# Attention and top-1 mixture of experts: written order on every engine, fixed weight buffers, later small loads, first unit loaded tile by tile

## Chip, cores and metric

The kernel runs on one core of one Trainium2 chip, in one launch. The metric is the device time in microseconds (us); of several runs it is the median. Engines are named as in the profile: PE (TensorE matmul), PEld (its weight load), DVE (VectorE), ACT (ScalarE), POOL (GpSimd), SP (SyncE, which here only issues DMAs).

## What is computed

Four batches of channel attention (a 256 x 256 softmax matrix per batch, taken over 3648 rows), and then every row goes to one of 16 experts, chosen by two argmax steps.

```
qn = q / (norm(q, axis=1) + 1e-6);  kn = k / (norm(k, axis=1) + 1e-6)     # B=4, N=3648, C=256
s = kn.transpose(0, 2, 1) @ qn / tau;  a = softmax(s, -1)                  # 256 x 256
x = (v @ a).reshape(B * N, C)                                              # 14592 rows
g_idx = argmax(x @ w_group);  e_idx = argmax(x @ w_expert[g_idx])          # 4 groups of 4 experts
out = (g_weight * e_weight) * (relu(x @ w1[g, e]) @ w2[g, e])              # F = 1024
```

## The kernel before

**Attention units.** A batch's 3648 rows are cut into 28 tiles of 128 rows and one of 64, and these into 8 units: seven of four tiles and a short one of one tile (`rows_of`, L150), so there are 32 units in all. An S unit adds its q and k tiles to the score matrix (`s_mm`, L193): three tiles as plain fp32 matmuls, the fourth (`SPLIT`) as three matmuls of rounded parts made by `s_split` (L167). `s_split` also squares the raw rows on ACT, and `s_add` (L186) adds the squares up on DVE. When a batch's S units are done, the generator `softmax` (L211) makes the attention matrix times [identity, routing weights], as two rounded parts `ahi`, `alo`. An X unit transposes four v tiles on PE (`x_tr`, L275), rounds them into `th` (ACT) and `tl` (DVE), and multiplies them (`x_mm`, L289); ACT copies the result to `xs`, DVE the 20 routing logits to `L`.

**Routing.** `routing` (L317) turns the logits of a range of tiles into slots, mostly on DVE with two small PE matmuls (`pp`). `scatter` (L391) has POOL write each tile's rows to their slots in device memory (`x_sorted`) with an indirect DMA, 116 of them, each followed by a small POOL memset (`pause`). X rows wait for this in a ring of `RING` = 10 buffers, which `xg` rows share.

**Experts.** 28 items of 512 rows of one expert each (`ffn1`, `ffn2`, L787 to L810; 8 steps an item, `lag` 2). The first `KPRE` = 4 items are full blocks found early, from the rows of batches 0 and 1 and the first 20 tiles of batch 2 (`PRE`); the others need the whole routing and its tables. The last 24 items also host small blocks ("q", L866 to L925). Weights come through three rotating buffers of one tag (`raw_tile`, L598) and are split into two rounded parts on ACT and DVE.

**Order.** The tile framework's scheduler orders instructions on each engine, with priorities given by hand (`high_priority` at L633, L707, L711). POOL goes by program order from the start (L622); all engines do from the 33rd step of the attention loop (L724) to the second expert step (L1022); then only SP and POOL. The attention loop (L721) runs S unit t beside X unit t - 10. q, k, v and the weights come on SP's queue; `tau` and the routing weights are five small DMAs on ACT's queue, issued first (L89 to L96). The first S unit comes in two halves (L162).

Of the kernel before, what the change touches and what calls it, by code (L numbers as in the profile page):

```python
# [17 lines left out]
P = 128  # L18
B, NT, C = 4, 3648, 256
N = B * NT  # L20
E = 16
# [16 lines left out]
KPRE = 4  # L38
# [5 lines left out]
RANGES = [[(0, 16), (16, NJ)], [(0, 16), (16, NJ)], [(0, 16), (16, 20), (20, NJ)], [(0, 16), (16, NJ)]]  # L44
# [8 lines left out]
XOFF = GPB + 2  # L53
TM = US
TURNS = (0, 1, 2, 3)
# [3 lines left out]
def attention_moe(ctx: ExitStack, tc, q, k, v, tau, w_group, w_expert, w1, w2, out):  # L59
# [29 lines left out]
    ACT.dma_start(tauc, tau[0:1, 0:1].broadcast_to([P, 1]))  # L89
    rtau = cp.tile([P, 1], F32, name="rtau")  # L90
    DVE.reciprocal(rtau, tauc)
    wcat = cp.tile([P, 2, NL], F32, name="wcat")
    for c in range(2):
        ACT.dma_start(wcat[:, c, 0:4], w_group[c * P:(c + 1) * P, :])
        ACT.dma_start(wcat[:, c, 4:NL].rearrange("p (g e) -> p g e", g=4),
                     w_expert[:, c * P:(c + 1) * P, :].rearrange("g p e -> p g e"))  # L96
# [9 lines left out]
    scms = {}  # L106
    for n in {j1 - j0 for r in RANGES for j0, j1 in r}:
        scms[n] = cp.tile([P, E * n], F32, name=f"scm{n}")
        DVE.memset(scms[n], 1.0)
        DVE.memset(scms[n].rearrange("p (e j) -> p e j", e=E)[:, :, 0:1], 0.0)  # L110
    carry = cp.tile([P, E], F32, name="carry")
    DVE.memset(carry, 0.0)
# [19 lines left out]
    DVE.tensor_tensor(part, part, slot1, ALU.add)  # L132
    zero = cp.tile([P, RW], F32, name="zero")
# [8 lines left out]
    vp = vp_.enter_context(tc.tile_pool(name="vp", bufs=3, side="right"))  # L142
# [15 lines left out]
    def s_load(u):  # L158
        rows, nj = rows_of(u % GPB)
        raw = spool.tile([P, 2, GJ, C], F32, tag="raw", name="qkraw", bufs=LOADS + 1)  # L160

        for j0, j1 in ((0, 2), (2, nj)) if u == 0 else ((0, nj),):  # L162
            for i, src in ((0, q), (1, k)):
                SP.dma_start(raw[:rows, i, j0:j1, :], tiles_of(src, u // GPB, u % GPB)[:, j0:j1, :])
        su[u] = dict(raw=raw)

    def s_split(u):  # L167
# [4 lines left out]
        if g < NG:  # L172
# [4 lines left out]
        if g == 0:  # L177
            d["acc"] = ps.tile([P, 2, C], F32, tag="acc", name="sacc")
            d["sqa"] = spool.tile([P, 2, GJ, C], F32, tag="sqa", name="sqa", bufs=1)
            ACT.activation(d["sqa"], raw, AF.Square)  # L180
        else:
            sq = spool.tile([P, 2, GJ, C], F32, tag="sq", name="sq")
            ACT.activation(sq[:rows, :, :nj, :], raw[:rows, :, :nj, :], AF.Square)  # L183
            x["sq"] = sq

    def s_add(u):  # L186
        b, g = divmod(u, GPB)
        if g:
            rows, nj = rows_of(g)
            sqa = st[b]["sqa"]  # L190
            DVE.tensor_tensor(sqa[:rows, :, :nj, :], sqa[:rows, :, :nj, :], su[u]["sq"][:rows, :, :nj, :], ALU.add)  # L191

    def s_mm(u):  # L193
# [3 lines left out]
        for j in range(nj):  # L197
            if j == SPLIT:
                hi, lo = x["hi"], x["lo"]
                terms = (hi, hi), (hi, lo), (lo, hi)  # L200
            else:
                t = x["raw"][:, :, j, :]
                terms = (t, t),
            for c in range(2):
                cs = slice(c * P, (c + 1) * P)
                for kt, qt in terms:
                    PE.matmul(d["acc"][:, c, :], kt[:rows, 1, cs], qt[:rows, 0, :],  # L207
                              start=d.pop("first", True) and c == 0, stop=(g == NG), skip_group_check=True)
                    d["first"] = False

    def softmax(b):  # L211

        d = st[b]
        ssq = ap_.tile([P, 2, C], F32, name="ssq", bufs=1)
# [3 lines left out]
        PE.matmul(nps[:, 0:C], onesf, ssq[:, 0, :], start=True, stop=False, skip_group_check=True)  # L218
        for c in range(2):
            PE.matmul(nps[:, C + c:C + c + 1], ssq[:, 1, c * P:(c + 1) * P], onesf[:, 0:1],  # L220
                      start=False, stop=True, skip_group_check=True)
        yield
        rn = ap_.tile([P, C + 2], F32, name="rn", bufs=1)
        ACT.activation(rn, nps[:, 0:C + 2], AF.Sqrt)
        DVE.tensor_scalar(rn, rn, 1e-6, None, ALU.add)
        DVE.reciprocal(rn, rn)
        DVE.tensor_scalar(rn[:, C:C + 2], rn[:, C:C + 2], rtau, None, ALU.mult)
        sm = ap_.tile([P, 2, C], F32, name="sm", bufs=1)
        for c in range(2):
            DVE.scalar_tensor_tensor(sm[:, c, :], d["acc"][:, c, :], rn[:, C + c:C + c + 1], rn[:, 0:C],  # L230
                                     ALU.mult, ALU.mult)
        mx = ap_.tile([P, 2], F32, name="mx")
        DVE.tensor_reduce(mx, sm, AX.X, ALU.max, negate=True)
        yield
        se = ap_.tile([P, 2], F32, name="se")
        for c in range(2):
            ACT.activation(sm[:, c, :], sm[:, c, :], AF.Exp, bias=mx[:, c:c + 1], accum_out=se[:, c:c + 1])
        DVE.tensor_scalar(se, se, 1e-9, None, ALU.add)
# [4 lines left out]
        yield  # L243
        yield
# [4 lines left out]
        yield  # L249
        aT = ap_.tile([P, 2, C], F32, name="aT", bufs=1)  # L250
        ACT.activation(aT.rearrange("p c n -> p (c n)"), atp, AF.Copy)
        yield
        yield
# [5 lines left out]
        yield  # L259
        DVE.tensor_copy(ax[:, :, C:NE], awp[:, 0:2 * NL].rearrange("p (c n) -> p c n", c=2))  # L260
        ahi = ap_.tile([P, 2, NE], F32R, name="ahi")
# [913 lines left out]
```

## Time and profile before

| | us |
|---|---|
| three runs | 963.89, 962.31, 960.90 (median 962.31) |
| profiled execution, its own time | 958.63 |
| its span, first to last instruction | 956.9 |
| outside the span | 1.73 |
| granted TensorE clock, mean | 0.994 |

The profile is one execution, 3.7 us under the median of the runs. Views give start times from the span's start. PE's busy time is modelled from its instructions, so two matmuls in a pipeline overlap in it; what a piece of PE work takes is read from the distance between starts.

### The profile page before, as it was taken

What the parts mean: (1) busy time and instruction counts of PE and PEld (TensorE: products, weight loads), DVE (VectorE), ACT (ScalarE), POOL (GpSimd) and SP (SyncE); (2) the same over time, 40 slices, a digit from 0 to 9 for tenths busy, and PEclk for the clock granted to TensorE, in tenths of its full rate; (3) what the DMA queues carried; (4) which work ended last, traced back from release to release, by engine and by line L of the source; (5) the groups of instructions that cost most, each with busy time, mean ns of one, the idle gap of its engine ahead of it and who ended that gap; (6) DMA issues with size and microseconds to landing.
All of it is one profiled execution on the core that took longest, in us unless ns stands there. A gap on an engine that the chain in (4) does not pass through costs nothing.

```text
span 956.9 us, 17625 instructions
## 1 busy us (share of the span) xinstructions
PE 924.3 (97%) x6238; PEld 809.5 (85%) x6238; DVE 750.0 (78%) x1511; ACT 477.3 (50%) x748; POOL 332.2 (35%) x425
## 2 busy tenths in 40 slices
PE   7999999988899999999999999999999999999995
PEld 6889899878799988888888888888888888888884
DVE  6989978798899977777877777778777877887731
ACT  6777768447554444444444444444443444444421
POOL 0003878878787322222111311232223222322121
PEclk9999999999999999999999999999999999999998
DMA  8866778448684545555566555666666666556500
GB/s 314 313 243 224 238 269 295 144 147 287 202 296 153 176 159 210 208 210 211 213 219 212 202 213 204 222 229 221 222 223 230 222 222 220 197 212 211 200 25 26
DMA packets 105585, 201.90 MB, mean 211 GB/s; under 512 B 10035, under 2 KB 64059, under 8 KB 105488
## 3 DMA queue, kind: packets, MB, share of 16 engines
q1 hardware_dynamic: 89056, 156.12, 47.6%
q0 software_dynamic: 14944, 44.54, 12.1%
q8 instruction: 51, 0.84, 0.3%
q14 instruction: 46, 0.38, 0.1%
q10 hardware_dynamic: 1488, 0.02, 0.1%
HBM read 170.33 MB, written 31.39 MB: 211 GB/s over the span
## 4 chain that ended last, share of the span: by engine, by line
PE 80%; DVE 6%; POOL 4%; issue 4%; DMA 2%; ACT 2%; POOLq 0%; SPq 0%; DVEq 0%; ACTq 0%
PE yacc L809 32%; PE hmm L793 32%; PE sacc L207 7%; POOL x_sorted L405 3%; PE qacc L913 2%; PE qmm L896 2%; PE xmm L303 2%; DMA qkraw<-in_k 2%; DVE sqa L191 1%; POOL pad L139 1%; PE vtr L284 1%; DMA x_sorted<-xs,si 1%; DVE vtl L286 1%; ACT sq L183 1%; PE qtr L903 1%
## 5 line engine op out<-in xcount | busy, mean ns | idle before, releaser
L797 ACT ACTIVATE hh<-hmm 128x512 fp32r<-128x512 f32 x224 | 133.4, 596 | 298.0 <-PE hmm L793 284.5
L819 POOL DMA_INDIRECT out<-ys,ids x112 | 111.1, 992 | 479.1 <-ACT ys L816 449.1
L809 PE MATMUL yacc<-wh,hh 128*128 128x256 f32 x896 | 256.2, 286 | 0.1
L809 PE MATMUL yacc<-wh,hl 128*128 128x256 f32 x896 | 252.5, 282 | 0.0
L809 PE MATMUL yacc<-wl,hh 128*128 128x256 f32 x896 | 252.0, 281 | 0.0
L798 DVE SCALAR_TENSOR_TENSOR hl<-hmm,hh 128x512 fp32r<-128x512 f32 x224 | 153.4, 687 | 85.9 <-ACT hh L797 84.3
L809 PEld LDWEIGHTS yacc<-wh,hh 128*128 128x128 f32 x896 | 168.7, 188 | 24.4 <-issue 15.0
L793 PE MATMUL hmm<-xth,wh 128*128 128x512 f32 x448 | 177.3, 396 | 0.0
L793 PE MATMUL hmm<-xth,wl 128*128 128x512 f32 x448 | 177.0, 395 | 0.0
L793 PE MATMUL hmm<-xtl,wh 128*128 128x512 f32 x448 | 176.8, 395 | 0.0
L809 PEld LDWEIGHTS yacc<-wl,hh 128*128 128x128 f32 x896 | 169.0, 189 | 8.2
L687 DVE STREAM_TRANSPOSE xt<-xg 32x256 f32<-32x256 f32 x384 | 167.2, 435 | 6.5 <-DMA xg<-x_sorted,ix_big 0.2
L640 DVE TENSOR_TENSOR wl<-wraw,wh 128x1024 fp32r<-128x1024 f32 x112 | 134.9, 1223 | 46.9 <-ACT wh L639 45.6
L809 PEld LDWEIGHTS yacc<-wh,hl 128*128 128x128 f32 x896 | 168.5, 188 | 0.0
L405 POOL DMA_INDIRECT x_sorted<-xs,si x116 | 135.6, 1169 | 56.3 <-issue 29.3
L639 ACT ACTIVATE wh<-wraw 128x1024 fp32r<-128x1024 f32 x112 | 116.2, 1055 | 74.1 <-DMA wraw<-in_moe_w 50.5
L793 PEld LDWEIGHTS hmm<-xth,wl 128*128 128x128 f32 x448 | 84.1, 188 | 19.9
L793 PEld LDWEIGHTS hmm<-xtl,wh 128*128 128x128 f32 x448 | 84.2, 188 | 11.0 <-DVE xtl L668 0.3
L793 PEld LDWEIGHTS hmm<-xth,wh 128*128 128x128 f32 x448 | 84.2, 188 | 9.7
L207 PE MATMUL sacc<-qkraw 128*128 128x256 f32 (+1 forms) x352 | 85.2, 388 | 6.0 <-DMA qkraw<-in_k 6.0
L207 PEld LDWEIGHTS sacc<-qkraw 128*128 128x128 f32 (+1 forms) x352 | 65.0, 193 | 14.6 <-DMA qkraw<-in_q 5.9
L303 PE MATMUL xmm<-ahi,vth 128*128 128x276 f32 (+1 forms) x232 | 69.7, 302 | 3.2 <-ACT ahi L263 1.8
(233 smaller groups left out, 1212.3 us busy)
## 6 DMA issues: line engine op xcount, KB each, us to landing
wraw<-in_moe_w SPq DMA_DIRECT2D x56, 1024.0 KB, 7.2
wraw<-in_moe_w SPq DMA_DIRECT2D x96, 512.0 KB, 5.4
vr<-in_v SPq DMA_DIRECT2D x28, 512.0 KB, 4.2
qkraw<-in_q SPq DMA_DIRECT2D x27, 512.0 KB, 4.8
qkraw<-in_k SPq DMA_DIRECT2D x27, 512.0 KB, 5.7
xg<-x_sorted SPq DMA_DIRECT2D x4, 544.0 KB, 4.0
x_sorted<-xs,si POOLq DMA_INDIRECT x116, 4.0
out<-ys,ids POOLq DMA_INDIRECT x112, 3.6
```

Of the source, the lines that this page charges most:

```text
L207: PE.matmul(d["acc"][:, c, :], kt[:rows, 1, cs], qt[:rows, 0, :], start=d.pop("first", True) and c == 0, stop=(g == NG), skip_group_check= ...
L303: PE.matmul(mm[:rows, :NE], vt[:, c, j * P:j * P + rows], at[:, c, :], start=(n == 0), stop=(n == 5))
L405: ins = POOL.indirect_dma_start(out=xs_d, out_offset=bass.IndirectOffsetOnAxis(ap=si[:rows, j:j + 1], axis=0), in_=xs[:rows, t, 0:RW].bitc ...
L639: ACT.activation(whs[n][:, s], raw[:, s], AF.Copy)
L640: DVE.tensor_tensor(wls[n][:, s], raw[:, s], whs[n][:, s], ALU.subtract)
L687: ins = DVE.transpose(xt[qs_, :, :, rs], xg[:, :, :, qs_])
L793: PE.matmul(mm, wt[:, c, fs], xt[:, c, :], start=(n == 0), stop=(n == 5))
L797: d["hh"] = ACT.activation(hh, mm, AF.Relu)
L798: d["hl"] = DVE.scalar_tensor_tensor(hl, mm, 0.0, hh, ALU.max, ALU.subtract)
L809: PE.matmul(a, ht[:, tsl], wt[:, f, :], start=(f == 0 and t % 2 == 0 and n == 0), stop=(f == 7 and n == 2), skip_group_check=True)
L819: ins = POOL.indirect_dma_start(out=out, out_offset=bass.IndirectOffsetOnAxis(ap=d["ids"][:, t:t + 1], axis=0), in_=ys[:, t, :], in_offset ...
L896: PE.matmul(mm[r, :], qs["xT"][q % 2][:, c, r], qs["w", p][:, c * 512:(c + 1) * 512], start=(c == 0), stop=(c == 1), tile_position=(0, p * ...
```

## The change

On all engines the program's order holds from the first attention unit to the end of the expert loop. Steps are cut finer and interleaved by hand: S and X tiles alternate, squares and their sums come in halves, `softmax` and `routing` yield a number of "hooks" (one hook after each tile) before they go on, and `take`/`give` keep two users of one PSUM buffer apart. X starts at unit 13 instead of 10, with two extra X-only steps (`ALONE`). The sum of squares ends in two additions instead of a reduction; the norms are 4 columns instead of 258 and are spread by a diagonal matmul; the copy of logits and part of the score scaling move from DVE to ACT; units 9 to 12 are not split. `KPRE` is 3 and `PRE` 16 tiles, batch 2 has three routing ranges. Weight buffers have fixed tags, the expert loop's DVE and ACT pieces follow a table (`PLAN`), and output scatters are held back until the fourth item's rows are asked for. `tau` and routing weights are loaded on SP at step 2, and the first unit comes as tile 0, tile 1, tiles 2 and 3, with q on SP and k on ACT.

```diff
-KPRE = 4
+KPRE = 3
+FLIP = 4
...
-RANGES = [..., [(0, 16), (16, 20), (20, NJ)], ...]
+RANGES = [..., [(0, 8), (8, 16), (16, NJ)], ...]
-PRE = (2, 20)
+PRE = (2, 16)
+VLOADS = 3
+UNSPLIT = (9, 10, 11, 12)
+FIRST = GPB + 5
+ALONE = (13, 15)
+HOP = 4
...
-    ACT.dma_start(tauc, tau[0:1, 0:1].broadcast_to([P, 1]))
...
+    def small_loads():
+        SP.dma_start(tauc, tau[0:1, 0:1].broadcast_to([P, 1]))
+        for c in range(2):
+            SP.dma_start(wcat[:, c, 0:4], ...)
+            SP.dma_start(wcat[:, c, 4:NL]..., ...)
...
-        for j0, j1 in ((0, 2), (2, nj)) if u == 0 else ((0, nj),):
+        for j0, j1 in ((0, 1), (1, 2), (2, nj)) if u == 0 else ((0, nj),):
             for i, src in ((0, q), (1, k)):
-                SP.dma_start(raw[:rows, i, j0:j1, :], ...)
+                (ACT if u == 0 and i else SP).dma_start(raw[:rows, i, j0:j1, :], ...)
...
-        DVE.tensor_reduce(ssq, d["sqa"].rearrange("p t j c -> p t c j"), AX.X, ALU.add)
-        yield
+        DVE.tensor_tensor(sqa[:, :, 0:2, :], sqa[:, :, 0:2, :], sqa[:, :, 2:4, :], ALU.add)
+        DVE.tensor_tensor(ssq, sqa[:, :, 0, :], sqa[:, :, 1, :], ALU.add)
+        yield hop
+        ACT.activation(tmp1, onesf[:, 0:1], AF.Sqrt)
+        while not take():
+            yield 1
...
+        ACT.activation(rn, nps[:, C:C + 4], AF.Sqrt)
+        ACT.activation(tmp1, zero[:, 0:1], AF.Exp)
...
-        DVE.tensor_copy(d["L"][:rows, g * GJ:g * GJ + nj, :], xs[:rows, :nj, C:NE])
+            ACT.activation(d["L"][:rows, g * GJ:g * GJ + nj, :], xs[:rows, :nj, C:NE], AF.Copy)
...
-    def raw_tile():
-        return wp.tile([P, 2048], F32, tag="wraw", name="wraw", bufs=3)
+    def raw_tile(n=None):
+        n = turn[0] % 3 if n is None else n
+        turn[0] += 1
+        return wp.tile([P, 2048], F32, tag=f"wraw{n}", name="wraw", bufs=1)
...
-        d[which + "r"] = t = raw_tile().rearrange("p (c f) -> p c f", c=n)
+        d[which + "r"] = t = raw_tile(0 if turn[0] > 9 else None).rearrange("p (c f) -> p c f", c=n)
...
-    ms.enter_context(tc.manual_schedule(engines={ET.Pool}))
+    ms.enter_context(tc.manual_schedule(engines={ET.Pool, ET.SP, ET.Activation, ET.PE, ET.DVE}))
...
+    def hook():
+        hooks[0] += 1
+        small.hook()
+        rgens.hook()
...
+    for n, (t, x) in enumerate(steps):
...
+        if n == 2:
+            small_loads()
...
+        if x == UX - 4:
+            while wp is None:
+                hook()
+            fetch_x(items[0], tb_pre, 0)
+        while x is not None and pend_of(x - RING + (x >= UX - 4)):
+            hook()
+            scatter(2)
...
+        for j in range(GJ):
+            if t is not None and j < rows_of(t % GPB)[1]:
+                s_tile(t, j)
...
+                hook()
+            if j == 0 and nx is not None:
+                x_tr(nx, 1)
+                hook()
+            if x is not None and j < rows_of(x % GPB)[1]:
+                x_tile(x, j)
+                hook()
...
+            if j == 1 and x == UX - 2:
                 split_x(items[0])
...
-        t = raw_tile()
+        t = raw_tile(1 + half)
...
+    PLAN = {(0, 0): range(0, 2), (0, 1): range(2, 4), (1, 0): ("w1", 0), (2, 0): ("w1", 1), (2, 1): range(4, 7),
+            (3, 0): range(7, 9), (3, 1): range(9, 12), (4, 0): range(12, 14), (4, 1): range(14, 16),
+            (5, 0): ("w2", 0), (5, 1): ("w2", 1), (6, 0): "x", (6, 1): "ids"}
...
+        if n == 8 * KPRE - 2:
+            split_x(items[KPRE])
...
+        if tb_big is not None and fetched is not None:
+            get(KPRE)
+            fetch_x(*where(KPRE + 1))
+            fetched = None
+            send()
```

## Rows read from the trace of the kernel before

**Rows 1.** The page's busy times of all engines over the span.

```profile
PE 924.3 (97%) x6238; PEld 809.5 (85%) x6238; DVE 750.0 (78%) x1511; ACT 477.3 (50%) x748; POOL 332.2 (35%) x425
```

**Rows 2.** Busy time by stretch: start:end length, each engine, clock, DMA, GB/s.

```profile
0.00:50.00 50.00, 44.03 (x230) 39.18 (x231) 39.66 (x60) 36.17 (x36) 1.57 (x12) 1.00 0.86 318
50.00:120.00 70.00, 66.69 (x469) 62.02 (x468) 63.17 (x121) 52.42 (x91) 30.93 (x41) 1.00 0.66 229
120.00:190.00 70.00, 67.79 (x469) 63.65 (x468) 54.79 (x107) 46.60 (x82) 56.76 (x82) 1.00 0.71 239
190.00:252.00 62.00, 53.21 (x383) 49.15 (x381) 53.49 (x177) 36.45 (x83) 48.17 (x82) 0.97 0.60 198
350.00:926.00 576.00, 576.00 (x3950) 490.54 (x3948) 443.93 (x794) 252.73 (x373) 130.15 (x127) 1.00 0.59 210
```

**Rows 3.** Chain that ended last, undisturbed attention step: start, length, what.

```profile
113.61 3.07 PE xmm L303 x24
116.68 0.87 PE vtr L284 x8
117.55 3.30 PE sacc L207 x18
```

**Rows 4.** Timeline of PE, first units, softmax, end: start, length, instruction.

```profile
5.97 4.58 PE L207 MATMUL sacc<-qkraw 128*128 128x256 f32 x12 [5.97 <-DMA qkraw<-in_k]
11.10 2.82 PE L207 MATMUL sacc<-qkraw 128*128 128x256 f32 x12
...
54.54 1.07 PE L257 MATMUL awp<-wcat,aT 128*128 128x20 f32 x8
...
250.12 1.09 PE L666 MATMUL xtr<-ident,xg 128*128 128x128 f32 x8 [1.09 <-DVE vtl L286]
...
251.81 0.39 PE L793 MATMUL hmm<-xth,wh 128*128 128x512 f32 x1
```

**Rows 5.** Timeline of SP's queue, the first loads.

```profile
0.81 0.41 SPq L164 DMA_DIRECT2D qkraw<-in_q  x1
1.28 0.43 SPq L164 DMA_DIRECT2D qkraw<-in_k  x1
...
4.78 0.33 SPq L164 DMA_DIRECT2D qkraw<-in_k  x1
```

**Rows 6.** Waits of SP's queue from 0 to 12: total us, times, longest.

```profile
SPq L164 <- DMA tauc<-in_tau: 2.6, 1, 2.6
```

**Rows 7.** Waits of PE from 0 to 252.

```profile
PE pp L359 <- DVE rs L357: 4.8, 6, 1.6
```

**Rows 8.** Groups of DVE from 0 to 252: busy us, mean ns, idle before.

```profile
L191 DVE TENSOR_TENSOR sqa<-sqa,sq 128x2048 f32<-128x2048 f32 (+1 forms) x28 | 57.5, 2054 | 4.1 <-ACT sq L183 3.7
...
L215 DVE TENSOR_REDUCE ssq<-sqa 128x512 f32<-128x2048 f32 x4 | 15.3, 3827 | 0.1
L309 DVE COPY L<-xs 128x80 f32<-128x80 f32 (+1 forms) x31 | 7.8, 252 | 9.5 <-ACT xs L306 9.4
```

**Rows 9.** Timeline of POOL and of DVE around 93, then an undisturbed scatter.

```profile
93.31 2.89 POOL L405 DMA_INDIRECT x_sorted<-xs,si  x1 [0.28 <-POOL xs L402]
...
98.29 0.97 POOL L405 DMA_INDIRECT x_sorted<-xs,si  x1 [0.17 <-issue]
...
93.05 2.28 DVE L191 TENSOR_TENSOR sqa<-sqa,sq 128x2048 f32<-128x2048 f32 x1
```

**Rows 10.** POOL's instructions on x_sorted alone, first and last quarter: busy (count).

```profile
85.95:144.37 58.42, 37.01 (x29) 1.00 0.77 258
...
250.15:298.00 47.85, 31.34 (x29) 1.00 0.76 259
```

**Rows 11.** Chain that ended last, one step of the expert loop.

```profile
361.43 1.44 PE yacc L809 x12
...
364.27 1.42 PE yacc L809 x12
```

**Rows 12.** The page's DMA issues: count, KB each, median us to landing.

```profile
wraw<-in_moe_w SPq DMA_DIRECT2D x56, 1024.0 KB, 7.2
```

More of the change, by code (lines that the diff above doesn't have):

```diff
@@ L196, in s_mm @@
         x, d = su[u], st[b]
[L197 to L209, printed above, removed]
+        if j == SPLIT and "hi" in x:
+            hi, lo = x["hi"], x["lo"]
+            terms = (hi, hi), (hi, lo), (lo, hi)
+        else:
+            t = x["raw"][:, :, j, :]
+            terms = (t, t),
@@ new lines, in s_tile, with take, give @@
+        for c in range(2):
+            cs = slice(c * P, (c + 1) * P)
+            for kt, qt in terms:
+                PE.matmul(d["acc"][:, c, :], kt[:rows, 1, cs], qt[:rows, 0, :],
+                          start=d.pop("first", True) and c == 0, stop=(g == NG), skip_group_check=True)
+                d["first"] = False
+    hooks, held = [0], [False, 0]
+    def take():
+        if held[0] or hooks[0] < held[1]:
+            return False
+        held[0] = True
+        return True
+    def give(n):
+        held[:] = [False, hooks[0] + n]
@@ L228, in softmax @@
+        DVE.tensor_tensor(dq, ident.unsqueeze(1).broadcast_to([P, 2, P]),
+                          rn[:, 0:2].unsqueeze(2).broadcast_to([P, 2, P]), ALU.mult)
+        yield hop
+        while not (d.get("scored") and take()):
+            yield 1
+        nps = ps.tile([P, 512], F32, tag="misc", name="nps", bufs=1)
+        PE.matmul(nps[:, 0:C], onesf, dq.rearrange("p c n -> p (c n)"), start=True, stop=True, skip_group_check=True)
         sm = ap_.tile([P, 2, C], F32, name="sm", bufs=1)
         for c in range(2):
-            DVE.scalar_tensor_tensor(sm[:, c, :], d["acc"][:, c, :], rn[:, C + c:C + c + 1], rn[:, 0:C],
-                                     ALU.mult, ALU.mult)
+            ACT.activation(sm[:, c, :], d["acc"][:, c, :], AF.Copy, scale=rn[:, 2 + c:3 + c])
@@ L314, in bc @@
+        ACT.activation(xs[:rows, j, :], mm[:rows, :NE], AF.Copy)
+        if j == nj - 1:
+            ACT.activation(d["L"][:rows, g * GJ:g * GJ + nj, :], xs[:rows, :nj, C:NE], AF.Copy)
+    scatters, pend, now, rows_at, early, gone = [], [], [0], {}, [], set()
     def bc(x, n):
@@ L364, in routing @@
         DVE.tensor_tensor(carry, pp[:, E:2 * E], carry, ALU.add)
+        give(HOP)
+        if (b, j1) == PRE:
+            DVE.tensor_copy(carried, carry)
+            small.gens.append(pre_gen())
         DVE.scalar_tensor_tensor(bs, bs, -1.0, ecap, ALU.add, ALU.add)
@@ L414, in scatter @@
             scatters.append(ins.ins)
+            if t == nj - 1:
+                gone.add((b, g))
             pause()
[L418 to L424 removed]
     def table_steps(items, cnt, start, held, stride, name):
@@ new lines, in pre_gen, with pend_of @@
+        yield HOP
+        wp = ctx.enter_context(tc.tile_pool(name="wp", bufs=4))
+        fetch_w(items[0], tb_pre, 0, "w1")
+        yield 10
+        fetch_w(items[0], tb_pre, 0, "w2")
+    def pend_of(u):
+        return any(rows_at.get(k) is not None and k not in gone for k in [divmod(w, GPB) for w in range(u + 1)])
+    steps, x = [], 0
+    for t in range(US):
+        steps.append((t, x if t >= FIRST else None))
+        x += t >= FIRST
+        if t in ALONE:
+            steps.append((None, x))
+            x += 1
```

545 lines of the change are left out of this document (294 added, 251 removed).

## Prediction

> **What bounds the kernel now.** I began with the page's busy times: PE is busy 97% of the span, DVE 78% [rows 1]. That average hides two stages, so the table of busy time by stretch came next [rows 2]. From 350 to 926 PE is busy all 576 us: nothing that leaves PE's instructions alone can gain there. All of PE's loss that a new order could recover lies in the attention stage, up to the first expert matmul at 251.81 [rows 4]. There DVE, at 63.2 of 70 us between 50 and 120, is nearly as full as PE, and in the last 62 us PE works only 53.2 [rows 2].
>
> How much is lost there I take from distances between starts, because modelled ends cover short gaps. An undisturbed step of one S and one X unit is 3.30 + 3.07 + 0.87 = 7.24 us [rows 3], and there are 28 such pairs of full units, 202.7. The four short S and X units cost about 1.9 a pair, 7.6 in all (an estimate: 4 fp32 matmuls at the 0.22 that 2.82 / 12 less the tail gives, six X matmuls between 250.97 and 251.81, two transposes). Each softmax has about 2.15 of PE work, of which `awp` is 0.9 [rows 4]; times four, 8.6. The first expert item's transposes take 0.85. Sum 219.8. PE needed 251.81 - 5.97 = 245.8 [rows 4], so **26.0 us are lost** behind the first matmul; 1.8 of these are the clock at its low level, with 12 matmuls in 4.58 instead of 2.82 [rows 4]. In front of it lie 5.97 us of waiting for the first loads.
>
> **Start.** SP's fourth load left only at 4.78, because its semaphore was still held by the `tau` load, a wait of 2.6 [rows 5, 6]. With the small loads moved behind step 1, the 1 MB of a unit flows without that hole. The first matmul now needs two pieces of 128 KB instead of 256 KB, k no longer issued 0.47 behind q [rows 5]. Bounds: 5.97 (nothing gained) and about 3.5 (fetch and landing shrink with the bytes in front); k landed 4.56 after its issue with 768 KB in flight, which at the 318 GB/s of that stretch [rows 2] is 2.4 of transfer, so with a third of that I take 4.5. Low-clock time I keep at 1.8, since in the trace it follows the first matmuls wherever they start; bounds 1 and 3.
> The Trainium skill (DMA: Bandwidth & Descriptors, "Issuing engines are not separate DMA queues") says that issuing from two engines saves only sequencer time, as the same 16 DMA engines carry both. By that rule the start would gain those 0.5 us and what smaller pieces give, some 5.3 instead of 4.5, and the sum below would be 0.8 worse; no row here separates the two.
>
> The small loads themselves, five issues of about 0.45 on SP at step 2, stand ahead of the loads of later units on that queue, 2.3 us; three units are loaded ahead (9.9 us of S work), which hides it. `rtau` is needed only in the first softmax.
>
> **Attention order.** PE's work stays: 219.8, plus four unsplit units at 16 plain matmuls instead of 12 plain and 6 rounded, about 0.15 each, 0.6. DVE loses the reduction of 3.83 a batch against two additions of about 1.8 together, the logits' copies of 7.8 us, four roundings of 0.7 and the reciprocal of 258 columns [rows 8]: about 8 + 8 + 3 + 6 = 25 of 210 us [rows 2]. ACT gains the copies, about 11 on 174 us; with 230 us of stage that is still 80%. So DVE no longer competes with PE in the pair steps. The waits that came from its backlog, such as 4.8 us of `pp` behind `rs` [rows 7], have a written distance of four hooks or more (an S unit, 3.3 us) instead. Finer alternation of fp32 and rounded matmuls costs nothing visible: the pair step's three pieces follow each other without a gap [rows 3].
> What remains lost? Zero is one bound, the present 24 the other. The nearest row is 120 to 190, where S, X, softmax and routing already ran together and PE missed 2.2 of 70 us [rows 2]; the first units after 5.97 missed none (44.03 of 44.03). At 2.2 per 70 the 177 us that are not S alone lose 5.6; I take 5.
> First expert matmul: 4.5 + 1.8 + 219.8 + 0.6 + 5 = **231.7**, 20.1 earlier.
>
> **POOL and the fourth item.** POOL's scatters set when items get their rows. Before, 116 took from 85.95 to 298 [rows 10], 1.83 each with waits. X unit 3, the first to allow routing, should end at about 73 (6.3 + 12 S units of 3.3 + 3.9 for the short unit, softmax and transposes + two pairs, one of them short, and two X-only steps), and 12 hooks later, at about 84, POOL starts. Item 0 needs 74 scatters, the fourth item (now the first that needs all tables) 116, at PE's step 22, 22 x 2.84 [rows 11] = 62 after the first expert matmul, 294. Without waits for slots a scatter's instruction took 1.28 in the first quarter and 1.08 in the last [rows 10] and about 0.5 more with its memset and issue [rows 9]: 58 x 1.77 + 58 x 1.57 = 194, so 278, plus about 9 (an estimate: gather issue and two landings, each well under the 7.2 of a 1 MB load [rows 12]): 287, in time. At the old 1.83 it is 305, and PE waits 11. Ranges come in pieces that keep POOL fed, so I am near the lower value: 1 us.
>
> **Expert stage.** From 251.81 on, 705.1 of the span; PE full, same matmuls. The new places of weight splits and 32 x 32 turns lie beside PE. A weight half now waits for its own buffer: w2 of an item goes into the buffer of w1, freed in step 2 and split in step 5, about 2.4 steps or 7 us for a load that lands in 7.2 [rows 12]. ACT may then stand up to a microsecond, with the relu of the next step behind it in its queue; PE reads that two steps (5.7 us) later. I take 0; bounds 0 and the rival below. The tail, 17 us behind the last expert matmuls, stays.
>
> **Sum.** 20.1 - 1 = 19.1. Against the profiled execution, 958.63 - 19.1 = 939.5; shifted by the 3.7 that the median of the runs lies higher, 943.2. I give 941 between the two. 0.3% of this, 2.9 us, is about what can be told from no change.
>
> **Rivals.**
> *POOL becomes the bound.* For it: a scatter beside an addition of squares took 2.89 instead of 0.97, the addition being 2.28 long [rows 9]; the additions stay, in halves, and each batch gets two more in place of a reduction; ring buffers make X units wait for scatters as well. Against it: the instruction gets short once S units are over [rows 10]. It decides once the mean is above 1.75. At 1.83 the wait is 11: gain 9, 949.5 to 953.
> The Trainium skill (SBUF — State Buffer, "SBUF: two separate sides") has the mechanism: VectorE with two SBUF inputs and GpSimd take one port pair in turn, and the loser waits for the whole instruction; the rows of 93 agree. By that rule eight new two-input additions, some 7 us, would push POOL's end back by as much, and the time would be about 946.
> *Everything is covered:* nothing lost but the low clock, 24 to 26 gained, 932 to 937. Against it: 20 small PE pieces (`pp`, `atp`, `awp`) that need a DVE result just made.
> *The order doesn't do what it says:* in a strict queue each late DMA or ACT result stops all behind it, so the 24 us return as other waits; time within 3 us of before. For it: DVE and ACT stay above 80%. Against it: the distances are written with two to four tiles of slack.
> *Slower:* one weight buffer in the expert stage. If w2 lands later than about 12 us after its buffer is free (7 to the split, 5 until PE needs what stands behind it), PE waits in each of the 24 hosted items; each microsecond costs 24. It turns the gain into a loss from 12.8 on; at 13 it is +5, 967. Against it: 7.2 median [rows 12] with the DMA engines at 59% [rows 2].
>
> **How the numbers follow.** Forecast with its bounds (own gain 12 to 24) 0.58; POOL 0.17; all covered 0.10; order without gain 0.08, of which 0.03 faster, 0.03 the same and 0.02 slower; weight buffer or another stall in each item 0.07, one seventh of it the same. Faster 0.88, same 0.04, slower 0.08. Range 932 to 954: from full cover to the POOL case on the median's scale.
>
> **What would show it.** Right: first matmul near 4.5; SP's fourth load without a wait; X unit 0 at about 50; first expert matmul at 229 to 235; no wait of PE for `rs`; step length 2.84 unchanged; no gap at the fourth item. Wrong: PE waiting for `xg` or for `xs` behind x_sorted in the last X units or at step 22 (POOL); expert items longer than before (weights); a first matmul near 5.5 or a longer low-clock stretch (start); DVE or ACT idle behind one late operand while PE waits (order).

## The result, and the profile after

| | before | after |
|---|---|---|
| median of four runs, us | 962.07 (960.90 to 963.89) | 950.11 (949.44 to 950.96) |
| profiled execution, us | 958.63 | 950.54 |
| its span, us | 956.9 | 948.8 |
| first matmul, us | 5.97 | 4.03 |
| unit 1 of S begins, us | 11.10 | 11.54 |
| first X matmul, us | 56.72 | 55.18 |
| first expert matmul, us | 251.81 | 244.68 |
| from there to the end of the span, us | 705.07 | 704.13 |

The ratio of the times is 0.9874, with a 95% interval of 0.9856 to 0.9893: the change makes the kernel 12.0 us faster. That lies inside the predicted range and beside the forecast: 941 was expected, a gain of about 20. In the two profiled executions the gain is 8.1, of which 7.1 lie in the attention stage, where 20.1 were expected; the other 3.9 of the 12.0 come from the comparison itself, since the profile of before was a quick execution of it (first experiment). So the forecast missed by more than the times show: 13.0 us at the first expert matmul, and these are to be explained.

The page of after, busy time and share of the span, against [rows 1]:

```profile
PE 927.7 (98%) x6246; PEld 812.0 (86%) x6246; DVE 749.5 (79%) x1502; ACT 484.2 (51%) x823; POOL 335.3 (35%) x426
```

Busy time by stretch (start:end, length, each engine with its instructions, granted clock, DMA share, GB/s), against [rows 2]:

```profile
0.00:50.00 50.00, 45.33 (x222) 39.50 (x223) 35.77 (x65) 35.42 (x48) 1.57 (x12) 1.00 0.89 318
50.00:120.00 70.00, 69.30 (x482) 64.71 (x481) 55.88 (x114) 55.11 (x112) 17.61 (x28) 1.00 0.61 213
120.00:190.00 70.00, 68.39 (x458) 63.40 (x457) 57.59 (x122) 50.63 (x105) 57.95 (x87) 0.98 0.71 248
190.00:244.00 54.00, 51.13 (x391) 47.81 (x390) 44.74 (x139) 39.07 (x100) 44.56 (x76) 1.00 0.61 202
350.00:918.00 568.00, 568.00 (x3895) 485.00 (x3893) 451.72 (x816) 247.66 (x370) 136.64 (x122) 1.00 0.61 211
```

Between 50 and 120, where VectorE was nearly as full as PE, it now works 55.9 us instead of 63.2, and PE misses 0.7 of 70 instead of 3.3. The last stretch, where PE worked 53.2 of 62, is now at 51.1 of 54. The third row has a clock of 0.98. From 350 on PE is full, as before. Where this table has no record of the granted clock it shows 1.00, so for the first microseconds the level is read from PE's pace: `sacc` matmuls on `qkraw` start 0.43 us apart at the low level and 0.22 at the full one.

The waits of PE in the whole span (line, what it waited for, us in total, times, longest), against [rows 7]:

```profile
PE sacc L226 <- DMA qkraw<-in_q: 4.7, 2, 4.0
PE vtr L335 <- DVE vtl L337: 2.6, 4, 1.3
PE pp L411 <- DVE rs L403: 1.3, 3, 0.5
PE atp L298 <- DVE carry L416: 0.8, 1, 0.8
```

The wait for `rs` has gone from 4.8 to 1.3. PE never waits for `xg`, so the fourth item begins without a gap, and behind `xs`, the ring buffers, it waits 0.2 at most. VectorE's rounding of the transposes (`vtl`) is now the largest single cause behind the start. The start, from PE's timeline (start, length, what, idle time before):

```profile
4.03 3.75 PE L226 MATMUL sacc<-qkraw 128*128 128x256 f32 x8 [4.03 <-DMA qkraw<-in_q]
8.42 2.04 PE L226 MATMUL sacc<-qkraw 128*128 128x256 f32 x4 [0.64 <-DMA qkraw<-in_q]
...
11.54 1.70 PE L226 MATMUL sacc<-qkraw 128*128 128x256 f32 x6
```

The first matmul is 1.94 earlier than in [rows 4], and unit 1 is 0.44 later. Tiles 3 and 4 of unit 0 came only at 8.4, and by their pace the matmuls ran at the low clock until 12.0 (before: 9.5).

POOL, the first scatter, the last one, and the gather of the fourth item's rows, against [rows 10]:

```profile
100.27 1.97 POOL L461 DMA_INDIRECT x_sorted<-xs,si  x1 [38.11 <-DVE qklo L184]
...
297.19 0.94 POOL L461 DMA_INDIRECT x_sorted<-xsr,si  x1 [1.97 <-issue]
...
302.48 1.05 POOL L537 DMA_INDIRECT xg<-x_sorted,ix_big  x1 [2.93 <-issue]
```

POOL starts 14 us later than before and ends at the same time.

### The profile page after: what moved, and what is told of

Its sections match the earlier page's. It is cut to its first block, busy times and chain, and to the rows that moved or that the text cites. A ratio compares the mean times of both kernels' runs of the same rounds, so it can differ in the third digit from the quotient of the medians.

```text
span 948.8 us, 17629 instructions
## 1 busy us (share of the span) xinstructions
PE 927.7 (98%) x6246; PEld 812.0 (86%) x6246; DVE 749.5 (79%) x1502; ACT 484.2 (51%) x823; POOL 335.3 (35%) x426
## 5 line engine op out<-in xcount | busy, mean ns | idle before, releaser
L941 POOL DMA_INDIRECT out<-ys,ids x112 | 127.8, 1141 | 454.2 <-ACT ys L928 423.0
L738 DVE TENSOR_TENSOR wl<-wraw,wh 128x1024 fp32r<-128x1024 f32 (+1 forms) x116 | 134.9, 1186 | 15.5 <-ACT wh L737 15.5
L461 POOL DMA_INDIRECT x_sorted<-xs,si x112 | 121.9, 1088 | 67.0 <-DVE qklo L184 38.3
L737 ACT ACTIVATE wh<-wraw 128x1024 fp32r<-128x1024 f32 (+1 forms) x116 | 115.5, 1023 | 0.0
L905 PEld LDWEIGHTS hmm<-xth,wl 128*128 128x128 f32 x448 | 84.1, 188 | 20.1
L226 PE MATMUL sacc<-qkraw 128*128 128x256 f32 (+1 forms) x368 | 95.1, 395 | 4.7 <-DMA qkraw<-in_q 4.7
L226 PEld LDWEIGHTS sacc<-qkraw 128*128 128x128 f32 (+1 forms) x368 | 67.9, 197 | 13.4 <-DMA qkraw<-in_k 5.3
L353 PE MATMUL xmm<-ahi,vth 128*128 128x276 f32 (+1 forms) x232 | 76.2, 328 | 0.2 <-ACT xs L356 0.2
```

The costliest lines, as they stand in the source:

```text
L353: PE.matmul(mm[:rows, :NE], vt[:, c, j * P:j * P + rows], at[:, c, :], start=(n == 0), stop=(n == 5))
L461: ins = POOL.indirect_dma_start(out=xs_d, out_offset=bass.IndirectOffsetOnAxis(ap=si[:rows, j:j + 1], axis=0), in_=xs[:rows, t, 0:RW].bitc ...
L737: ACT.activation(whs[n][:, s], raw[:, s], AF.Copy)
L738: DVE.tensor_tensor(wls[n][:, s], raw[:, s], whs[n][:, s], ALU.subtract)
L905: PE.matmul(mm, wt[:, c, fs], xt[:, c, :], start=(n == 0), stop=(n == 5))
L941: ins = POOL.indirect_dma_start(out=out, out_offset=bass.IndirectOffsetOnAxis(ap=d["ids"][:, t:t + 1], axis=0), in_=d["ys"][:, t, :], in_o ...
```

## The experiments

Runs of one kernel on one chip differ by up to 5 us with this program, on one chip by 11 (the kernel before, 964.58 to 975.54), so first the kernel before was profiled again. Each ratio below is to the kernel before on the same chip; medians of two experiments can come from two chips.

**The kernel before, again** (no edit).

> The kernel before once more, to see whether its profiled execution (958.63, span 956.88) is typical of its runs (960.9 to 963.89). If executions scatter by 3 us, this profile lies anywhere between 958 and 964, and its first expert matmul lies as much later than 251.81 as the time is above 958.63. If the profiled execution always lies below, it comes out at 958 to 959 again.

Measured: 961.02 (959.0 to 962.93), ratio 1.0001 (0.9986 to 1.0016). Profiled execution 960.88, span 959.1, first expert matmul at 253.08, 706 from there to the end. So it is scatter, not a steady shift: of the 2.2 us between the two spans 1.3 arise up to the first expert matmul and 1.0 behind it. A part in front is the clock: the first profile has one stretch at the low level there (207.5 to 210.9), this one two (208.4 to 211.8 and 218.6 to 222.0), and 3.4 us at half speed cost 1.7. The prediction's profile lies 2.4 to 3.4 us below the middle of the runs, while after's lies 0.4 above it.

**First unit as before** (everything else as after).

```
-        for j0, j1 in ((0, 1), (1, 2), (2, nj)) if u == 0 else ((0, nj),):
+        for j0, j1 in ((0, 2), (2, nj)) if u == 0 else ((0, nj),):
...
-                (ACT if u == 0 and i else SP).dma_start(raw[...], ...)
+                SP.dma_start(raw[...], ...)
```

> The kernel after, with the first unit loaded as before: two halves, all four transfers on SP (the small loads stay behind step 1). The prediction's term for the start says: first matmul at 5.5 to 6 instead of 4.03, unit 1 begins later than 11.54 by 1 to 1.5, time 951 to 951.5. Rival, from the trace of after: the early first matmul buys nothing, because the pieces of 1 KB a row bring less per us and the hole of 0.64 keeps the clock low until 12.0. Then the first matmul is at 5.6 to 6, unit 1 begins at 10.5 to 11.1, and the time is 0.4 to 1 lower, 949.1 to 949.7.

Measured: 947.95 (947.51 to 948.17), ratio 0.9864 (0.9839 to 0.9889), below both expectations. PE's timeline:

```profile
4.45 5.46 PE L226 MATMUL sacc<-qkraw 128*128 128x256 f32 x12 [4.45 <-DMA qkraw<-in_k]
...
10.71 2.75 PE L226 MATMUL sacc<-qkraw 128*128 128x256 f32 x12
```

Both expectations for the first matmul were wrong: 512 KB in two halves let it start at 4.45, against 5.97 in before. Its two loads are issued at 0.81 and 1.28 in both kernels, ahead of SP's wait [rows 5, 6], and the loads in front differ only by the small ones on ScalarE's queue. The table by stretch, before and then this kernel:

```profile
2.00:3.50 1.50, 0.00 (x0) 0.00 (x0) 0.45 (x5) 0.00 (x0) 0.23 (x2) 1.00 0.29 70
2.00:3.50 1.50, 0.00 (x0) 0.00 (x0) 0.00 (x0) 0.30 (x2) 0.23 (x2) 1.00 0.83 292
```

With the small loads in front the DMA engines are busy 29% of this time, without them 83%. So moving them is worth 1.5 us at the first matmul, by these two kernels; no run moves them alone, and why so few bytes hold the others back the rows don't show. The tile-by-tile load brings the first matmul another 0.4 forward and unit 1 0.83 back. The rival holds for unit 1. The first expert matmul is at 242.03, 2.65 earlier than in after: 0.83 from the start, and 1.8 behind it, about the price of the stretch at the low clock that is missing here. After has it from 152.0 to 155.4, behind a wait of PE for `carry` of 0.78 that ends at 149.45; here the same wait, 0.83 and ending at 148.44, is followed by none. First after's windows, then this kernel's:

```profile
148.00:152.00 4.00, 3.22 (x24) 2.56 (x22) 3.83 (x10) 2.54 (x8) 1.19 (x3) 1.00 0.91 362
152.00:156.00 4.00, 4.00 (x16) 3.57 (x15) 3.86 (x14) 1.35 (x3) 1.80 (x3) 0.58 0.00 0
```

```profile
147.00:151.00 4.00, 3.17 (x23) 2.52 (x21) 3.83 (x10) 2.46 (x8) 0.00 (x0) 1.00 0.79 321
151.00:155.00 4.00, 4.00 (x28) 3.79 (x28) 3.86 (x15) 2.14 (x5) 1.81 (x3) 1.00 0.15 19
```

In four us PE gets through 16 matmuls at a granted clock of 0.58 and through 28 at 1.00. The two runs of after with a mean clock of 0.996 took 949.44 and 949.67, the two with 0.994 took 950.54 and 950.96.

**First unit by tiles, on SP alone** (the other half of that edit).

```
-                (ACT if u == 0 and i else SP).dma_start(raw[...], ...)
+                SP.dma_start(raw[...], ...)
```

> The kernel after, first unit tile by tile as there, but all six transfers on SP's queue. This tells the pieces' size from the second queue. If the second queue is the loss (the trace of after has k's last 256 KB on ScalarE's queue trickling in at 12 to 49 kB per us from 5 to 8 us, while SP's queue already brings unit 1), unit 1 begins at 10.2 to 10.9 and the time is that of the kernel with two halves on SP, 947.5 to 948.5. If the small pieces of 1 KB a row are the loss, unit 1 begins at 11.1 to 11.7 and the time stays at 949 to 950.5.

Measured: 948.39 (947.78 to 949.93), ratio 0.987 (0.9853 to 0.9887). PE's timeline:

```profile
3.78 4.88 PE L226 MATMUL sacc<-qkraw 128*128 128x256 f32 x12 [3.78 <-DMA qkraw<-in_k]
...
10.53 1.32 PE L226 MATMUL sacc<-qkraw 128*128 128x256 f32 x5 [1.16 <-DMA qkraw<-in_k]
```

So the second queue makes the loss, not the small pieces. With one queue the first matmul is at 3.78, a quarter of a us earlier than with two, and there is no hole between tiles 2 and 3. With two, k's last 256 KB took 6.4 us from issue to landing, since SP's queue had gone on to unit 1 and shared the DMA engines with it; on SP's queue the same piece took 3.8. The Trainium skill (DMA: Bandwidth & Descriptors, "Queues, rings and completion order") has each DMA engine take the queues in turn, a packet at a time; these two numbers agree. Here PE finishes unit 0 at 9.2 and stands 1.16 for k of unit 1.

Not all of the 1.0 us at unit 1 (10.53 against 11.54) is the queue. In after PE does not wait there: it is late itself, after the third tile's late arrival and at the low clock. Two kernels below keep its two queues and reach the full clock earlier, the doubled memset and the planner's order; their unit 1:

```profile
11.24 1.10 PE L227 MATMUL sacc<-qkraw 128*128 128x256 f32 x4 [0.16 <-DMA qkraw<-in_k]
10.95 1.32 PE L226 MATMUL sacc<-qkraw 128*128 128x256 f32 x5 [0.26 <-DMA qkraw<-in_k]
```

With two queues and no added matmuls unit 1 thus begins at 10.95 to 11.54 in three traces, with one queue at 10.40 to 10.71 in seven.

**Matmuls ahead of the data.** Products of a constant tile ahead of unit 0, to have the clock up when the data come. First version: 13 ahead, 24 between the second and third tile.

```
...
+            if n == 0 and j in (0, 2):
+                warm(j)          # 13 or 24 times matmul(wmp, onesf, onesf)
...
```

> The kernel after, with 13 matmuls on a constant tile ahead of unit 0 and 24 between its second and third tile, whose product is multiplied by zero. If the low clock up to 12.0 is what holds the start, the granted clock rises at 4.5 to 5.5, unit 1 begins at 10.3 to 10.8 instead of 11.54, and the time is 0.8 to 1.2 lower. If the arrival of the third and fourth tile (8.4) and of unit 1 is the bound, unit 1 begins no earlier than 11.2 and the time is the same within 0.4.

Measured: 952.30 (952.0 to 953.17). The edit was sized wrongly: an fp32 product of 128 columns is two passes, which start 0.213 apart at the low clock and 0.111 at the full one, so the added work itself held unit 0 until 6.27 and its third tile until 13.36. Nothing follows on the clock but that it was full by 5.6. From unit 1 on (14.94) to the first expert matmul (246.25) it took 231.31, as with the first unit as before (231.32): the start only shifts what follows. Second version, 8 products, with the first unit in two halves on SP:

> The kernel after with the first unit in two halves on SP, and 8 matmuls of 128 columns on a constant tile ahead of unit 0 (two passes of 0.204 each at the low clock, measured in the run with 13: 1.13 + 3.3 = 4.4, just before the data at 4.45). Clock theory: the granted clock is full from about 5.6 instead of 10.4, unit 1 begins at 9.1 to 9.6 instead of 10.71, and the time is 1.1 to 1.6 below that of the two halves alone (947.95), 946.3 to 946.9. Transfer theory: PE then waits for unit 1 or 2, the gain is under 0.5, 947.4 to 948.4.

Measured: 947.62 (947.0 to 947.9), ratio 0.9856 (0.9839 to 0.9872). PE's timeline:

```profile
1.14 3.78 PE L833 MATMUL wmp<-onesf 128*128 128x128 f32 x16 [1.14 <-DVE onesf L86]
4.71 2.13 PE L226 MATMUL sacc<-qkraw 128*128 128x256 f32 x8
7.98 1.10 PE L226 MATMUL sacc<-qkraw 128*128 128x256 f32 x4 [1.14 <-DMA qkraw<-in_k]
...
10.54 1.32 PE L226 MATMUL sacc<-qkraw 128*128 128x256 f32 x5 [0.34 <-DMA qkraw<-in_k]
```

The clock was full at 5.2 instead of 10.4, unit 0's first eight matmuls took 2.1 instead of some 3.8, and all of it went into waits for k: unit 1 begins at 10.54. The clock theory falls. With two quite different starts unit 1 begins at 10.53 and 10.54, both times behind a wait for its own k: there that transfer is the bound. The first unit as before comes within 0.2 of it, and after's execution lies 1.0 above.

**The order given back to the planner** in the attention stage; operations, buffers and POOL's order as in after.

```
-    ms.enter_context(tc.manual_schedule(engines={ET.Pool, ET.SP, ET.Activation, ET.PE, ET.DVE}))
+    ms.enter_context(tc.manual_schedule(engines={ET.Pool}))
...
+    ms.close()
+    ms.enter_context(tc.manual_schedule(engines={ET.Pool, ET.SP, ET.Activation, ET.PE, ET.DVE}))
     while len(quarters) > 3:
```

> The kernel after, with the order of SP, ScalarE, PE and VectorE left to the planner again up to the last X unit, as in before; the operations, the ranges, the buffers and POOL's order are those of after. If the written order is what took the stalls away, they come back: first expert matmul at 251 to 257 instead of 244.7, time 957 to 962. Rival: the gain comes from VectorE's lighter load (squares in halves added without a reduction, logits copied by ScalarE) whatever the order; then the first expert matmul is at 243 to 247 and the time 948.5 to 952.5.

Measured: 954.59 (952.07 to 955.51), ratio 0.9928 (0.9905 to 0.9950), between the two expectations. First expert matmul at 249.00. PE's waits:

```profile
PE pp L411 <- DVE rs L403: 5.7, 2, 3.6
PE sacc L226 <- DMA qkraw<-in_q: 5.1, 2, 3.8
PE sacc L226 <- DVE qklo L184: 1.3, 4, 0.3
```

The wait for `rs` is back at 5.7, and its trace has two stretches at the low clock (116.0 to 119.4, 177.4 to 180.8). So of the 12 us about 5 are the written order (4.5 by the medians, 5.2 by the ratios), one more stretch at the low clock than in after included. The other 7 come from what the two kernels share: the lighter VectorE, the new start, the finer steps and the changes in the expert stage. This run does not tell these apart.

**A fixed order on the kernel before.**

```
-TM = US
+TM = 0
```

> The kernel before with one change: all five engines go by the program's order from the first unit on (there it begins only at the 33rd step), with before's places in the program, whole-unit steps and no written distances. If the fixed order by itself is the gain, the time falls to 950 to 957. If the gain lies in the distances of four hooks and the finer mixing of S and X tiles, PE stands behind softmax and routing results, the first expert matmul comes at 258 to 285 and the time is 965 to 992.

Measured: 1012.43 (1009.93 to 1015.97), where the kernel before ran at 968.97 on the same chip; ratio 1.0452 (1.0384 to 1.0520), further up than expected. The edit does more than its expectation says: `TM` also has three pieces of the routing run inside each X unit, where five ran behind it. First expert matmul at 300.49. PE's waits:

```profile
PE nps L218 <- DVE ssq L215: 15.7, 4, 4.4
PE atp L248 <- DVE ax L242: 11.4, 4, 8.2
```

Each softmax stops PE for the reduction of 3.7 us and again for the exponentials' scaling. So a fixed order of before's steps, without written distances, is a loss of 4.5%. Whether the distances, the removal of the long VectorE operations or the finer steps make a gain of it was not taken apart.

**POOL's memset twice** behind each scatter.

```
         POOL.memset(pad, 0.0)
+        POOL.memset(pad, 0.0)
```

> The kernel after with POOL's small memset behind each scatter done twice, some 0.35 to 0.4 more for each of 116 scatters. If POOL is only just in time (last gather of the fourth item's rows at 302.5, PE at it at 306.7), the 74 scatters from 176 on, where POOL runs without a pause, put the rows 20 to 28 later and the time rises by 16 to 26, to 966 to 976, with a wait of PE at the fourth item or in the last X units. If POOL has the slack that the forecast gave it (16 us and more by its numbers, 13 of them in the scatters' own waits), the time rises by less than 8.

Measured: 1018.23 (1017.79 to 1018.68), ratio 1.0591 (1.0570 to 1.0612): 68 more, far above even the expectation of a POOL with no slack. The second memset cost more than its own 0.31: scatters follow each other every 2.12 us instead of 1.48, 0.64 more and not 0.35 to 0.4, which is 74 us over 116 of them. PE's waits:

```profile
PE xmm L354 <- ACT xs L357: 31.1, 8, 11.3
PE xtr L767 <- DMA xg<-x_sorted,ix_big: 20.4, 1, 20.4
```

The expectation had named both waits, for 16 to 26 us together. The X units wait 31.1 in eight pieces, because ScalarE can't copy rows into a ring buffer (`xs`) before POOL has scattered it (ScalarE's own waits for that are 42.9); and PE, standing in pieces, ran at a mean clock of 0.80 between 200 and 300. So a slower POOL stops PE in two places; how near after is to it, the next experiment shows.

**Longer distances**: `HOP` 6 instead of 4, with the first unit in two halves on SP.

```
-HOP = 4
+HOP = 6
...
             while "alo" not in st[x // GPB]:
+                hooks[0] += 1
                 small.hook()
```

> The kernel after with the first unit in two halves on SP and the written distance HOP between an operation and PE's use of its result raised from 4 to 6 hooks (softmax and routing; the loop that waits for a softmax now counts its hooks). If the remaining waits of PE come from distances that are too short (1.3 for rs, 0.8 for carry, some more behind vtl), these go, the first expert matmul comes at 239.5 to 241 instead of 242.0 and the time is 945.5 to 947. Rival: the routing chain gets longer by 2 to 4 hooks a range, X has to wait for ring buffers or POOL's rows for the fourth item come after PE is there (slack 4); then the waits of PE behind scatters or xg grow and the time is 948 to 956.

Measured: 957.35 (957.02 to 957.86), ratio 0.9958 (0.9942 to 0.9975). PE's waits:

```profile
PE xtr L766 <- DMA xg<-x_sorted,ix_big: 2.6, 1, 2.6
PE xmm L353 <- ACT xs L356: 2.0, 1, 2.0
PE vtr L335 <- DVE vtl L337: 1.8, 1, 1.8
...
PE pp L411 <- DVE rs L403: 0.3, 1, 0.3
```

The rival holds, and the time lies beyond its range. The waits for `rs` and `carry` do go, all but 0.3, but the gather of the fourth item's rows comes at 307.8 instead of 300.1. The first and the third item take 4 us longer each; in the third these are the wait of 2.6 at its end and a stretch of 3.4 at the low clock behind it. The kernel loses 9.4 against the same start with `HOP` 4.

**Longer distances with a short memset** (8 columns instead of 256), to see whether POOL's rate is what forbids them.

```
-        POOL.memset(pad, 0.0)
+        POOL.memset(pad[:, 0:8], 0.0)
```

> The kernel with HOP 6 and the first unit in two halves on SP (957.35 without this edit), with POOL's memset behind each scatter on 8 columns instead of 256, so that a scatter's period falls by some 0.2 to 0.3. If the longer distances cost time only because POOL's rows come late (waits 2.0 for ring buffers, 2.6 and more at the fourth item, 4.1 longer in that item), these go, the fourth item begins on time (third step 22.6 again) and the time is 948 to 951, or 945.5 to 947 if the first item's extra 4.0 goes with them. If the extra 4.0 of the first item comes from VectorE's later tables (weights of the first item fetched and split later), it stays, and the time is 950 to 953. If POOL is not the reason, 956 to 958.

Measured: 1013.83 (1013.11 to 1014.17) beside 968.97 of before; ratio 1.0453 (1.0391 to 1.0514). No theory had this. The scatters follow each other every 1.28 us instead of 1.48. Up to 380 us PE, VectorE and ScalarE now have 26.5, 7.9 and 5.9 us of idle time for which no wait is on record, where `HOP` 6 with the whole memset has none; they rarely stand at the same time. PE at 136:

```profile
135.79 0.16 PE L256 MATMUL nps<-onesf,ssq 128*128 128x1 f32 x1
136.89 0.25 PE L256 MATMUL nps<-onesf,ssq 128*128 128x1 f32 x1 [0.94 <-issue]
137.62 0.16 PE L256 MATMUL nps<-onesf,ssq 128*128 128x1 f32 x1 [0.47 <-issue]
```

These are passes of one group on the same operands, which follow each other 0.11 apart in the other kernels. Whether the longer distances would pay with a quicker POOL stays open, because this edit doesn't make POOL quicker: its last scatter starts at 330.2 instead of 299.7.

**The norms of before**, with the first unit in two halves on SP.

```
-        for i in range(4):
-            PE.matmul(nps[:, C + i:C + i + 1], ssq[:, i // 2, ...], onesf[:, 0:1], ...)
+        PE.matmul(nps[:, 0:C], onesf, ssq[:, 0, :], start=True, stop=False, ...)
+        for c in range(2):
+            PE.matmul(nps[:, C + c:C + c + 1], ssq[:, 1, c * P:(c + 1) * P], onesf[:, 0:1], ...)
...
-        DVE.tensor_tensor(dq, ident..., rn[:, 0:2]..., ALU.mult)
-        PE.matmul(nps[:, 0:C], onesf, dq..., start=True, stop=True, ...)
```

> The kernel after with the first unit in two halves on SP (947.95), and the norms computed as in before: one product of the constant tile with the q sums, two columns for k, root and reciprocal over 258 columns on VectorE (1.76 instead of 0.18), no diagonal tile. PE then has 1.7 us less work in all (per batch 4 passes of 0.108 instead of 8, and 2 of 0.216 either way), VectorE 4.8 more. If PE's work is what sets the stage, the first expert matmul comes at 240.2 to 240.6 instead of 242.0, time 946.1 to 946.8. If VectorE is as near the bound as PE, the 1.7 are given back as waits and the time is 947.5 to 950.

Measured: 958.86 (957.3 to 960.34) beside 968.97 of before, ratio 0.9883 (0.9824 to 0.9942), too wide to say anything. So once more, on another chip:

> The kernel with the norms of before once more, since the kernel before ran at 964.6 to 975.5 on the chip of the first run, against 959 to 964 on the others. The first run's trace has the wait of the transposes (atp) for carry at 1.9 instead of 0.8, and the clock at its low level for 10.2 us from 148.4 on and for 3.4 from 216.6, 6.8 us of work lost. If that stall belongs to the kernel (VectorE's reciprocal over 258 columns makes carry late), it is there again, the first expert matmul comes at 243 or later and the time is 948.5 to 958. If it belonged to the chip, the 1.7 of saved PE work show: first expert matmul at 240.2 to 241.5, time 946.1 to 947.5.

Measured: 947.90 (947.35 to 951.13), ratio 0.9866 (0.9839 to 0.9893), the same as without the edit (947.95); first expert matmul at 242.35 instead of 242.03, between the two expectations. PE's waits:

```profile
PE vtr L331 <- DVE vtl L333: 3.1, 5, 1.6
PE pp L407 <- DVE rs L399: 1.8, 3, 0.8
PE atp L294 <- DVE carry L412: 1.4, 1, 1.4
```

Each of the three has grown (from 2.7, 1.3 and 0.8): the saved PE work comes back as waits for VectorE. The longer low clock of the first run did not come again. One execution of each kernel is compared here, but it points to a price of VectorE's time in the stage: 4.8 us more of it cost PE about as much as the saved passes bring.

## Why the prediction was right in the sign and off in the size

**Start: wrong in a term that was kept.** The first matmul came at 4.03 against 4.5, but the sum's next term, 1.8 for the low clock, was 4.2 with the wait of 0.64 for the third tile: unit 0 took 7.5 us instead of 3.3. Unit 1 began at 11.54, not at 9.6, so 1.9 of the missing 13 us are here. The step that failed was to take the first matmul for the end of the start. Its end is unit 1, which with one queue began at 10.40 to 10.71 in seven traces, with the first matmul anywhere from 3.78 to 4.71. How long the low clock lasts differs too: with the same two queues it ended at 12.0 in after, at 7.9 with the doubled memset and at 6.7 under the planner. Of the SP term the gain is right and the reason is not: the wait of 2.6 is gone, but it held back the second half of k, for which PE in before has no wait [rows 4]; the 1.5 that the first unit in two halves shows are the first two loads landing earlier. The Trainium skill (DMA: Bandwidth & Descriptors, "Issuing engines are not separate DMA queues") was the better guide on the second queue, though not with the 5.3 worked out from it: the runs show that two queues bring nothing, and at unit 1 cost 0.2 to 1.1 against one.

**PE's work: 1.3 too low.** "PE's work stays" overlooked the norms. Before, a batch's norms were one product over 256 columns and two of one column; now they are four of one column and one over 256 columns from a diagonal tile, each in two passes. By the distances of their starts the 40 passes take 4.7 us, the 24 of before 3.4 with their waits. It can't be had back by undoing it, as the norms run shows.

**Other losses: 14.7 instead of 5.** This is the largest error, 9.7 of the 13: from unit 1 on, 244.68 - 11.54, less the 218.4 of work that is left of 219.8 + 0.6 + 1.3 without unit 0. 1.8 of it is one stretch at the low clock in this execution; the first unit as before has none, and its loss is 12.9. There ten waits of 0.35 to 1.7 make 6.9: behind `vtl` at 202, 208, 217 and 235, behind `rs` at 110, 168 and 183, behind `carry` at 147, and two more at 80 and 210. The other 6.0 are in pieces under 0.25, and some of that may be work that the sum left out, since it was built on a single undisturbed step; this stays open. The forecast had scaled up the 2.2 of 70 from [rows 2], a stretch without the tail's tables. In the tail VectorE has the last routings, the tables and the weights' splits ahead of `vtl`. That longer distances would help there is not shown: with six hooks PE still waits 1.8 behind `vtl` in one piece. The relief of VectorE was mis-sized too: it works 194.7 us up to the first expert matmul instead of 210.9, 16 less and not 25. The squares in halves cost 60.4 us instead of 57.5 [rows 8], and the diagonal tile and the added operations of the new softmax were not counted. ScalarE's 11 more came out at 9.4 (180.9 instead of 171.5, for which the forecast had 174).

**POOL: right that it is no bound, for a wrong reason.** First scatter forecast at 84, last at 278, rows at 287; measured 100.3, 297.2 and about 306.3 (the gather's instruction at 302.5; its 557 KB pass the DMA engines from 304.0 on). X unit 0 began at 55.2 instead of 50 (1.9 from the start; the rest, not measured apart, from step 13's own first S tile and transposes, the unsplit tiles and the norms), X unit 3 ended at 78.3 instead of 73, and the routing behind it took 16.6 us from VectorE's first reduction to the last reciprocal, not 11. The fourth item's transposes came at 308.8: 2.5 us to spare. Had the first expert matmul come at 231.7 with POOL as it was, those transposes would have stood at 295.8, and some 10.5 us of the gain would have been handed back (an estimate from these rows, and an upper one: POOL's chain depends on the same units, and in the first unit as before the first expert matmul came 2.65 earlier and the gather 2.4). So 231.7 needed a POOL chain that this kernel did not have. The Trainium skill's rule (SBUF — State Buffer, "SBUF: two separate sides") did not decide: a scatter took 1.09 us on the mean of 112, and POOL lost its time before the first one.

**Expert stage: nearly right.** 704.13 instead of 705.1. Items 2 and following take what they took (25.3, 25.1, 24.69, 24.71), so the single weight buffers cost nothing and the rival on the slower side fell. The first item is 0.95 shorter, which no step had: in before PE stood there 0.7 in front of the routing's `pp` at 261.4, for VectorE, and 0.25 in its first two matmuls, and after has neither.

**Median and profile.** The 3.7 between before's profiled execution and its median was kept as a shift for both kernels. It was chance: before's second profile lies 0.1 below the median of its runs, after's 0.4 above. Against the median the gain is 12.0, against the profile 8.1.

**The rivals.** "Everything is covered" fell by 13 us. "POOL becomes the bound" did not happen, but was 2.5 us away, and that the kernel ended in the time it named for 1.83 a scatter, 949.5 to 953, is a coincidence. "The order doesn't do what it says" holds in part: without the order the kernel is at 954.6, so more than half of the gain is not the order's.

**A better version?** The first unit in two halves on SP, alone or with 8 products ahead of it, took 947.95 and 947.62. Against before these are ratios of 0.9864 and 0.9856 beside 0.9874, with intervals that overlap; after's trace and theirs differ by 0.8 to 1.0 us at unit 1, in part by the clock, and no more than that is claimed.

## What to carry to other kernels

Where a start is cut into pieces, follow it to the second unit's first matmul: here the first matmul moved by 1.9 us and unit 1 by 0.4 the other way, in part because a second queue only shared the same transfers. A written order needs distances between an operation and the use of its result, but each distance lengthens the chain that feeds the next engine (six hooks instead of four cost 9.4 us), so sum that chain (X, routing, scatters, gather) with the new times in front of it before booking the gain. Take the loss that remains from the worst stretch, not from the best one, and ask of a profiled execution where it stands among its runs.

## What the runs showed of the hardware that was not expected

- **The low clock doesn't follow from the wait alone.** PE waits for `carry` at the same place in four kernels. A wait of 0.78 up to 149.45 was followed by the low level for 3.4 us in after; 0.83 up to 148.44 in the first unit as before by none; 1.41 up to 148.22 in the second norms run by none, and 1.94 up to 148.67 in the first went with 10.2 us of it from 148.4 on. Each 3.4 us at 1.2 GHz cost 1.7. After's four runs follow the mean clock, but before's do not: on one chip its runs at a mean of 0.994 took 959.26 to 963.18. What decides was not found.
- **A shorter memset behind each scatter made the kernel slower by 5%.** At a period of 1.28 us instead of 1.48 PE stood up to 9 us without a wait on record, POOL's idle time without a cause before its scatters grew from 24.9 to 86.6 us, and the ratio to before rose from 0.9958 to 1.0453. The memset's 256 columns were the only difference, and they look like waste. That the scatters' rate is the reason was not shown: the trace has no row for what is short then, and no other period was tried. A second memset of 0.31 in its turn lengthened the period by 0.64.
- **The same transfer took longer on a second queue.** k's last 256 KB took 6.4 us on ScalarE's queue beside SP's, 3.8 on SP's own.
